# Holding back the first transposing DMA of a gated mixer kernel, and 256 more warm-up columns on TensorE

## The chip, the cores and the metric

The kernel runs on one core of a Trainium2 chip. Its time is the device time of one execution in microseconds (us); a kernel is compared with another by the medians of runs on the same chip. Separately, one execution is profiled. Its rows count from the start of the program's first instruction, so a row "at 5.61" starts 5.61 us into the span.

## The reference

Three results are computed from the same x (2048 tokens by 512) and mixed: an attention with 32 heads over 8 earlier tokens at distance 2, a mixer that works over the tokens (w1 and w2 multiply along the sequence), and a gate per token.

```python
qkv = x @ wqkv                          # 512 -> 3 x 512, 32 heads of 16
idx = pos[:, None] - 2 * arange(8)      # the 8 tokens that a token looks at
logits = einsum("bhsd,bhswd->bhsw", q, kg) / 4
a = (softmax(logits) . vg) @ wo
u = gelu(einsum("bsd,sf->bdf", layernorm(x), w1) + b1)    # f = 1792
b = (einsum("bdf,fs->bds", u, w2) + b2).transpose
g = sigmoid((x * gate_w).sum(-1))
out = g * a + (1 - g) * b
```

## The kernel before

The kernel lists its work as operations with an engine, an estimated duration and names that they read and write. A planner (`_Sched`, L72) puts them into one fixed order for each engine and works out which semaphores each must wait for. An operation in `deps` of another is waited for; one in `order` only comes ahead of it in the plan. SP issues nearly all loads, and an instruction that waits on SP holds back everything that stands behind it there. The field `lands` of a load is only an estimate that the planner orders by.

TensorE runs five stages in this order: the q, k and v projections (L617, four 128x512 matmuls for a tile of 128 columns by 512 tokens), with the attention logits' head sums between them (L696), the first half of the token mixer (L810), the second half (L860), and the output projection (L876). ScalarE takes the results out of PSUM (L625 and L628 for q, k and v), VectorE forms the attention products, the softmax and the weighted sums, and the last steps on VectorE (L897) mix the two branches before the result is stored.

The projections need x transposed. Its tokens are cut into four blocks of 512. Blocks 1 to 3 are transposed by DMAs (`ld_xt`, L457, issued at L460). Block 0 is brought in two ways, since the first matmuls wait for it:

- Columns 0 to 127 are loaded untransposed by a 128 KB load into the tile XP (`d_xp`, L479, issued by ScalarE at L429). Four small TensorE matmuls with an identity transpose them (`f_tr`, L540, matmuls at L544); ScalarE (L553) and VectorE (L555) each copy half of the result into the tile XT.
- Columns 128 to 511 are transposed by a DMA (`ld_xt0`, L470, issued by SP at L473).

The weights of q come in four 128 KB pieces, one for each 128 rows. The first, `d_wp0_0`, is issued by ScalarE behind `d_xp`; the other three, the two 256 KB halves of k's weights, the first rows of x and the transposing DMA of block 1 follow `ld_xt0` on SP. All this is the list `first_loads` (L481), whose dependences are cleared, so that none of these loads waits for anything in the kernel before.

The projections of block 0 are split into passes. First comes a pass over the first 128 rows for four banks of PSUM (four matmuls, needing the TensorE transposes and `d_wp0_0`), then a pass over the second 128 rows (needing `ld_xt0` and the second piece of q's weights), and so on (L633 to L639).

TensorE has nothing to do until then. It multiplies constants into a bank that is not read: five 512-column matmuls (warm1, L548), one of 256 columns (warm2), then the four transposes, then one of 512 columns (warm3, L552); all of them are the matmuls at L536. The first projection matmul is ordered behind warm3 (w3_, L639).

VectorE's first operation, `rp` (L426, instruction at L424), adds up columns of the identity that GpSimd makes at L417; its result is read by the head sums much later.

Of the kernel before, what the change touches and what calls it, by code (L numbers as in the profile page):

```python
# [333 lines left out]
def bass_gated_mix__sliding_local_dilated__mixer_token_mlp__prompt_kernel(nc, A_x, A_wqkv, A_wo, B_x, B_w1, B_b1, B_w2, B_b2, gate_w, out, dbg=None):  # L334
    with contextlib.ExitStack() as es:
# [79 lines left out]
        A = sch.add  # L415
# [7 lines left out]
            with nc.allow_low_precision(reason="exact 0/1 indicator sums"):  # L423
                return e.tensor_reduce(out=RP, in_=sub(IDENT, 0, [(4, 32), (1, 4)]), axis=AX.X, op=ALU.add)  # L424

        A("dve", f_rp, 0.2, reads=["ident"], writes=["rp"], name="rp")  # L426

        def mk_dma(dst, src):
            return lambda e: e.dma_start(dst, src)  # L429
# [3 lines left out]
        def throttle():  # L433
            return [init_dmas[-5]] if len(init_dmas) >= 5 else []

        def prev_dma():
            return [init_dmas[-1]] if init_dmas else []

        def ld_x(t0, n, q="sp"):
            ds = sch.dsem("x%d" % t0)  # L440
            op = sch.dma(q, mk_dma(X[:, t0:t0 + n, :], xv[:, t0:t0 + n, :]), n * 128 * D * 2, ds,
                         writes=["x%d" % t for t in range(t0, t0 + n)], deps=throttle() if q == "sp" else [], after=prev_dma() if q == "sp" else [], name="d_x%d" % t0)
            if q == "sp":
                init_dmas.append(op)
            return op

        def ld_w(tn, d0, n, q="sp"):
            ds = sch.dsem("wqkv%d_%d" % (tn, d0))
            op = sch.dma(q, mk_dma(WQKV[:, d0:d0 + n, tn * D:(tn + 1) * D], wqkv_v[:, d0:d0 + n, tn * D:(tn + 1) * D]),
                         n * 128 * D * 2, ds, writes=["wqkv%d_%d" % (tn, dt) for dt in range(d0, d0 + n)],  # L450
                         deps=throttle() if q == "sp" and n == 4 else [], after=prev_dma() if q == "sp" else [],
                         issue=0.65 if n == 4 else 0.45, name="d_wp%d_%d" % (tn, d0))
            if q == "sp":
                init_dmas.append(op)
            return op
# [11 lines left out]
        def xt_of(sb, d0=0, d1=4):  # L467
            return XT0[d0:d1] + (XT0[4:] if d0 == 0 else []) if sb == 0 else ["xt_%d" % t for t in range(4 * sb, 4 * sb + 4)]

        def ld_xt0():  # L470
            ds = sch.dsem("xt0")
            dst = XT[:, 1:4, 0:512]
            op = sch.dma("sp", lambda e: e.dma_start_transpose(dst, x2d[0:512, 128:512]), 512 * 384 * 2, ds, issue=1.25,  # L473
                         writes=XT0[1:4], after=prev_dma(), name="d_xt0")
            init_dmas.append(op)
            return op
# [4 lines left out]
        first_loads = [ld_w(0, 0, 1, "act"), ld_xt0(), ld_w(0, 1, 1), ld_w(0, 2, 1), ld_w(0, 3, 1), ld_w(1, 0, 2), ld_w(1, 2, 2),  # L481
                       ld_x(0, 2)]
        ld_xt(1)
        first_loads.append(init_dmas[-1])
        for op_, t_ in zip(first_loads, (3.4, 4.6, 5.0, 5.4, 5.8, 6.6, 7.4, 8.2, 10.6)):
            op_.lands = t_
            op_.deps.clear()
        d_xp.lands = 3.1
        first_loads[0].order.add(d_xp)
        init_dmas[:] = [first_loads[1]] + first_loads[5:]  # L490
        ld_x(2, 2)
        ld_x(4, 4)
# [7 lines left out]
        def ld_w1(j):  # L500
# [4 lines left out]
            if j < 4:  # L505
# [8 lines left out]
                       writes=["wo"], deps=throttle(), after=prev_dma(), name="d_wo")  # L514
# [4 lines left out]
        for i_, (v_, n_) in enumerate(((B_b1, NFT), (B_b2, NST))):  # L519
            vr = v_.rearrange("(t q j) -> q t j", q=4, j=32)  # L520
            for q_ in range(4):
                sch.dma("sp", mk_dma(psub(BR, 32 * q_, n_, 32 * i_, [(1, 32)]), vr[q_]), n_ * 64, ds_b, reads=["br"],
                        writes=["br_%d_%d" % (i_, q_)], deps=throttle(), after=prev_dma(), name="d_b_%d_%d" % (i_, q_), issue=0.45)
        d_w1.append(ld_w1(3))
        A("dve", lambda e: e.transpose(out=BT, in_=BR), 0.2, reads=["br_%d_%d" % (i_, q_) for i_ in range(2) for q_ in range(4)],
          writes=["btc"], name="t_b")
# [5 lines left out]
        def f_warm(n, w_=D):  # L532
            def fn(e):
                ins = None
                for _ in range(n):
                    ins = e.matmul(ps[:, 7, 0:w_], lhsT=CONE[:, 0:128], rhs=CONE[:, 0:w_], start=True, stop=True)  # L536
                return ins
            return fn

        def f_tr(h):  # L540
            def fn(e):
                ins = None
                for t in range(2):
                    ins = e.matmul(ps[:, 5 + h, 128 * t:128 * t + 128], lhsT=XP[:, 2 * h + t, :], rhs=IDENT, start=True, stop=True)  # L544
                return ins
            return fn
# [2 lines left out]
        w2_ = A("pe", f_warm(1, 256), 0.2, writes=["lg7_0", "lg7_1"], name="warm2", prio=-100)  # L549
        ta_ = A("pe", f_tr(0), 0.215, reads=["outs0", "ident"], writes=["lg5_0", "lg5_1"], after=[w2_], name="tr0", prio=-100)  # L550
        tr_ = A("pe", f_tr(1), 0.215, reads=["outs0", "ident"], writes=["lg6_0", "lg6_1"], after=[ta_], name="tr1", prio=-100)
        w3_ = A("pe", f_warm(1), 0.43, writes=["lg7_0", "lg7_1"], after=[tr_], name="warm3", prio=-100)  # L552
        A("act", lambda e: e.activation(out=XT[:, 0, 0:256], in_=ps[:, 5, 0:256], func=AF.Copy), 0.35, reads=["lg5_0", "lg5_1"],  # L553
          writes=["xt0_0"], name="ev_tra", prio=0)
        A("dve", lambda e: e.tensor_copy(out=XT[:, 0, 256:512], in_=ps[:, 6, 0:256]), 0.35, reads=["lg6_0", "lg6_1"],  # L555
          writes=["xt0_0b"], name="ev_trb", prio=0)
# [12 lines left out]
        for hf in range(2):  # L569
            t0 = 8 * hf  # L570
            for t in range(t0, t0 + 8):
                A("dve", (lambda t_: (lambda e: e.bn_stats(out=ST6[:, t_, :], in_=X[:, t_, :])))(t), 0.59,  # L572
                  reads=["x%d" % t], writes=["st6_%d" % t], name="ln1_%d" % t, prio=0)
# [13 lines left out]
              reads=["zc%d" % hf], writes=["sd%d" % hf], name="ln_sqrt%d" % hf, prio=0)  # L587
            A("dve", (lambda t0_: (lambda e: e.reciprocal(out=cols(RSTD, t0_, 8), in_=cols(SD, t0_, 8))))(t0), 0.25,
              reads=["sd%d" % hf], writes=["rstd%d" % hf], name="ln_rstd%d" % hf, prio=0)
# [43 lines left out]
        for (b0, d0, d1, s0, s1) in ((0, 0, 1, 0, 512), (0, 1, 2, 0, 512), (0, 2, 3, 0, 512), (0, 3, 4, 0, 512), (4, 0, 2, 0, 512), (4, 2, 4, 0, 512)):  # L633
            for b in range(b0, b0 + 4):
                tn, dl = first[b]
                last_main[0] = A("pe", f_proj(tn, dl, 0, b, d0, d1, s0, s1), 0.216 * (d1 - d0) * (s1 - s0) / 512,
                                 reads=xt_of(0, d0, d1) + ["wqkv%d_%d" % (tn, dt) for dt in range(d0, d1)],
                                 writes=fbn[b], after=[last_main[0]], name="pf_%s%d_%d_%d" % (tnames[tn], dl, d0, s0))
                last_main[0].order.add(w3_)  # L639
        for b, (tn, dl) in enumerate(first):  # L640
            A("act", f_evq(tn, dl, 0, b), 0.52, reads=fbn[b] + (["k5pad"] if tn == 1 else []),
              writes=["%s5_%d_0" % (tnames[tn], dl)], name="ev_%s%d_0" % (tnames[tn], dl), prio=0)
# [7 lines left out]
        for (tn, dl, sb) in seq_proj:  # L650
# [3 lines left out]
                             reads=xr + ["wqkv%d_%d" % (tn, dt) for dt in range(4)],  # L654
                             writes=["acc%d" % bank], after=[last_main[0]], name="pj_%s%d_%d" % (tnames[tn], dl, sb), prio=0)
            A("act", f_evq(tn, dl, sb, bank), 0.62, reads=["acc%d" % bank] + (["k5pad"] if tn == 1 else ["v5pad"] if tn == 2 else []),
              writes=["%s5_%d_%d" % (tnames[tn], dl, sb)], name="ev_%s%d_%d" % (tnames[tn], dl, sb), prio=0)
# [11 lines left out]
                writes=["xa"] + ["wqkv%d_%d" % (tn, dt) for tn in range(3) for dt in range(4)], name="d_xa")  # L669
        for t in range(NST):  # L670
# [5 lines left out]
          writes=["th"], name="g_tanh", prio=0)  # L676
        A("dve", lambda e: e.tensor_scalar(out=G, in0=TH, scalar1=0.5, scalar2=0.5, op0=ALU.mult, op1=ALU.add), 0.15,
          reads=["th"], writes=["g"], name="g_g", prio=0)
        A("dve", lambda e: e.tensor_scalar(out=OMG, in0=TH, scalar1=-0.5, scalar2=0.5, op0=ALU.mult, op1=ALU.add), 0.15,
          reads=["th"], writes=["omg"], name="g_omg", prio=0)  # L680
        A("dve", lambda e: e.tensor_tensor(out=C2, in0=OMG, in1=B2C, op=ALU.mult), 0.15,
          reads=["omg", "b2c"], writes=["c2"], name="g_c2", prio=0)
# [25 lines left out]
        for wh in range(2):  # L708
# [6 lines left out]
            for (dl, c0, nc_) in pieces:  # L715
# [3 lines left out]
                  reads=["q5_%d_%d" % (dl, sb) for sb in range(c0, c0 + nc_)] +  # L719
                        ["k5_%d_%d" % (dl, sb) for sb in range(max(c0 - 1, 0), c0 + nc_)] + ["k5pad"],  # L720
                  writes=wr, name="qkm_%d_%d_%d" % (wh, dl, c0), prio=0)
            rd = sum([pbn(b_) for b_ in bufs], []) + PBX[wh] + ["rp"]
            for wl in range(4):
                qop = A("pe", f_qkr(list(enumerate(bufs)), (wl,)), 0.92, reads=rd, writes=["lg%d_0" % (4 + wl), "lg%d_1" % (4 + wl)],
                        name="qkr_%d_%d" % (wh, wl), prio=-100 + wl, delay=BURST_DELAY)
                A("act", (lambda wh_, wl_: (lambda e: e.activation(out=ATT[:, :, 4 * wh_ + wl_, :], in_=ps[:, 4 + wl_, :].rearrange("p (h c) -> p h c", h=2), func=AF.Copy)))(wh, wl),  # L726
                  0.55, reads=["lg%d_0" % (4 + wl), "lg%d_1" % (4 + wl)], writes=["lw%d" % (4 * wh + wl)],
                  name="lev_%d_%d" % (wh, wl), prio=0)
# [24 lines left out]
        for hf in range(2):  # L753
# [3 lines left out]
              reads=["outs1"], writes=["lh%d" % hf] + (wall if hf == 0 else []), name="sm_sub%d" % hf, prio=0)  # L757
            if hf == 0:
                A("act", lambda e: e.activation(out=col(SD, 0), in_=col(ZC, 0), func=AF.Exp, scale=0.0), 1.5,
                  reads=["zc0"], writes=["sd0"], name="sm_pre")  # L760
            A("act", (lambda hf_, l_: (lambda e: e.activation(out=ATT[:, hf_], in_=l_, func=AF.Exp)))(hf, lgh), 1.95,  # L761
              reads=["lh%d" % hf], writes=["att%d" % hf], name="sm_exp%d" % hf, prio=0)
        for hf in range(2):
# [5 lines left out]
            def f_rcp(e, hf_=hf):  # L769
# [6 lines left out]
              reads=["rs%d" % hf], writes=["att%d" % hf], name="sm_nrm%d" % hf, prio=0)  # L776
# [4 lines left out]
        for u in range(8):  # L781
            c, hf = u // 2, u % 2
            ds_at = sch.dsem("atx%d" % u)
            for a_ in range(4):
                dst = bass.AP(ATX.tensor, ATX.offset + a_ * pst + u * NW * HC, [[4 * pst, 32], [1, NW * HC]])
                sch.dma("act", mk_dma(dst, psub(ATT, 32 * c, 32, hf * NW * HC, [(1, NW * HC)])), 32 * NW * HC * 2, ds_at, issue=0.62,
                        reads=["att%d" % hf], writes=["atx_%d_%d" % (u, a_)], deps=pb_readers, name="d_atx_%d_%d" % (u, a_))
        USEQ = [0, 2, 1, 3, 4, 6, 5, 7]
        for k_, u in enumerate(USEQ):
# [6 lines left out]
              reads=v_res + ["atx_%d_%d" % (u, a_) for a_ in range(4)], writes=[pn] + [qk_res, k_all][k_ % 2], name="avm_%d" % u)  # L796
            for (nm, n_, du) in (("ava", 4, 2.25), ("avb", 2, 1.2)):
                A("dve", (lambda pv_, n__: (lambda e: e.tensor_tensor(out=pv_[:, 0:n__], in0=pv_[:, 0:n__], in1=pv_[:, n__:2 * n__], op=ALU.add)))(pv, n_),  # L798
                  du, writes=[pn], name="%s_%d" % (nm, u))
# [27 lines left out]
        for ft in range(NFT):  # L827
# [5 lines left out]
              reads=["acc%d" % bank, "b1c"], writes=["ut%d" % ft] + ALLXT,  # L833
              name="gel_%d" % ft, prio=0)
# [84 lines left out]
        for i in range(NST):  # L919
# [4 lines left out]
            elif i > 1:  # L924
# [5 lines left out]
              reads=["acc%d" % bank, "omg", "c2"], writes=["t1_%d" % i, "x%d" % i],  # L930
              name="t1_%d" % i, prio=0)
# [119 lines left out]
```

## Time and profile before

| what | value |
|---|---|
| time, median of 3 runs | 168.18 us (167.72 to 168.53) |
| the profiled execution's own time | 168.55 us |
| its span, first to last instruction | 167.3 us |
| TensorE busy (matmuls) | 162.1 us, 97% of the span |
| VectorE busy | 151.3 us, 90% |
| ScalarE busy | 75.1 us, 45% |
| GpSimd busy | 0.7 us |
| mean DMA rate over the span | 177 GB/s |
| first projection matmul starts | 5.61 us |
| last matmul ends | about 165.1 us (L876) |

The profile names an engine's instructions by line: PE is TensorE, PEld its weight loads, DVE VectorE, ACT ScalarE, POOL GpSimd, SP the engine that issues loads. SPq and ACTq rows are DMA issues, and the time in such a row is how long the issue took, not the transfer. Queue q1 in the DMA view belongs to SP and q10 to ScalarE.

### The profile page before, as it was taken

The page shows a single profiled execution, that of the slowest core. Times are in us where ns is not written, and L with a number is a line of the kernel's source. Part 1 is how long each engine was busy: PE and PEld are TensorE (multiplying, and loading weights), DVE is VectorE, ACT ScalarE, POOL GpSimd, SP SyncE. Part 2 cuts the span into 40 slices and gives each one's busy share as a digit, 9 for nine tenths or more (in the row PEclk, how much of TensorE's full clock was granted, in tenths as well). Part 3 has the DMA queues.
Part 4 walks back from the last instruction along what each step waited for, and adds up shares of the span by engine and source line. Part 5 has one row for each costly group of instructions (what it writes and reads, how often), then busy time and mean ns, then how long its engine had stood idle before and what let it go on. Part 6 is the DMA issues. An engine that isn't in the chain of part 4 may idle for free.

```text
span 167.3 us, 2136 instructions
## 1 busy us (share of the span) xinstructions
PE 162.1 (97%) x845; PEld 77.5 (46%) x859; DVE 151.3 (90%) x154; ACT 75.1 (45%) x116; POOL 0.7 (0%) x8
## 2 busy tenths in 40 slices
PE   7699999999999999999999999999999999999994
PEld 2355555554454444444444444444444444444463
DVE  1055999999999999999999999999999999999896
ACT  3077688889899818793131121131231321310100
POOL 1000000000000000000000000000000000000000
PEclk9999999999999999999999999999999999999999
DMA  5999999959003846996779926462672570000454
GB/s 135 327 268 216 314 316 290 303 165 308 2 0 97 311 116 179 307 290 155 181 189 340 339 76 142 113 187 71 181 218 83 138 223 0 0 0 0 157 190 159
DMA packets 47625, 29.64 MB, mean 177 GB/s; under 512 B 9856, under 2 KB 46464, under 8 KB 47616
## 3 DMA queue, kind: packets, MB, share of 16 engines
q1 hardware_dynamic: 45120, 24.85, 54.4%
q10 hardware_dynamic: 2496, 4.66, 10.2%
q8 instruction: 7, 0.11, 0.3%
q14 instruction: 2, 0.02, 0.0%
HBM read 21.24 MB, written 2.10 MB: 140 GB/s over the span
## 4 chain that ended last, share of the span: by engine, by line
PE 91%; DMA 3%; DVE 2%; ACT 2%; issue 1%; ACTq 0%
PE ps L860 29%; PE ps L810 29%; PE ps L617 23%; PE ps L876 6%; PE ps L696 4%; DMA arena<-in_A_wqkv_dram 3%; DVE arena L897 2%; ACT L585 1%; ACT arena L628 1%; ACTq L429 0%; ACT arena L585 0%
## 5 line engine op out<-in xcount | busy, mean ns | idle before, releaser
L860 PE MATMUL ps<-arena 128*128 128x512 bf16 x220 | 48.5, 379 | 0.2
L810 PE MATMUL ps<-arena 128*128 128x512 bf16 x219 | 48.2, 379 | 0.4 <-issue 0.2
L617 PE MATMUL ps<-arena 128*128 128x512 bf16 x188 | 41.4, 379 | 1.6 <-DMA arena<-in_A_wqkv_dram 1.3
L688 DVE TENSOR_TENSOR arena<-arena 128x4096 bf16<-128x4096 bf16 (+1 forms) x12 | 35.5, 2998 | 2.5 <-ACT arena L628 2.1
L795 DVE TENSOR_TENSOR arena<-arena 128x8192 bf16<-128x8192 bf16 x8 | 35.0, 4419 | 0.0
L860 PEld LDWEIGHTS ps<-arena 128*128 128x128 bf16 x224 | 21.9, 98 | 26.4
L810 PEld LDWEIGHTS ps<-arena 128*128 128x128 bf16 x224 | 21.8, 98 | 26.6 <-ACT arena L726 0.4
L617 PEld LDWEIGHTS ps<-arena 128*128 128x128 bf16 x192 | 21.6, 113 | 21.5 <-issue 1.8
L928 ACT ACTIVATE arena<-ps,arena 128x512 bf16<-128x512 f32 x16 | 12.5, 778 | 39.4 <-PE ps L860 39.4
L798 DVE TENSOR_TENSOR arena<-arena 128x4096 bf16<-128x4096 bf16 (+1 forms) x16 | 27.0, 1751 | 0.0
L628 ACT ACTIVATE arena<-ps 128x512 bf16<-128x512 f32 x32 | 18.6, 596 | 4.5 <-PE ps L617 4.5
L831 ACT ACTIVATE arena<-ps,arena 128x512 bf16<-128x512 f32 x14 | 9.6, 687 | 22.2 <-PE ps L810 16.6
L572 DVE BATCH_NORM_STATS2 arena<-arena 128x6 f32<-128x512 bf16 x16 | 10.0, 682 | 6.1 <-DMA arena<-in_A_x_dram 6.1
L876 PE MATMUL ps<-arena 128*128 128x512 bf16 (+1 forms) x79 | 14.1, 336 | 0.1
L897 DVE SCALAR_TENSOR_TENSOR arena<-ps,arena 128x512 bf16<-128x512 f32 (+1 forms) x20 | 11.5, 637 | 0.9 <-PE ps L876 0.7
L596 ACT ACTIVATE arena<-arena 128x512 bf16<-128x512 bf16 x16 | 12.2, 804 | 0.0
L625 ACT ACTIVATE arena<-ps 128x512 bf16<-128x512 f32 x16 | 9.0, 597 | 6.2 <-PE ps L617 6.1
L876 PEld LDWEIGHTS ps<-arena 128*128 128x128 bf16 x80 | 7.8, 98 | 6.2
L672 DVE SCALAR_TENSOR_TENSOR arena<-arena 128x512 bf16<-128x512 bf16 x16 | 10.1, 689 | 0.0
L742 DVE TENSOR_TENSOR arena<-arena 128x512 bf16<-128x512 bf16 (+4 forms) x11 | 7.3, 667 | 0.6 <-ACT arena L761 0.2
L696 PE MATMUL ps<-arena 128*32 128x512 bf16 x128 | 7.3, 380 | 0.0
L726 ACT ACTIVATE arena<-ps 128x512 bf16<-128x512 f32 x8 | 4.7, 592 | 4.6 <-PE ps L696 4.6
(42 smaller groups left out, 40.0 us busy)
## 6 DMA issues: line engine op xcount, KB each, us to landing
arena<-in_B_w_dram SPq DMA_DIRECT2D x7, 1024.0 KB, 8.5
arena<-in_B_w_dram SPq DMA_DIRECT2D x8, 896.0 KB, 5.2
arena<-arena ACTq DMA_DIRECT2D x32, 128.0 KB, 2.9
arena<-in_A_x_dram SPq DMA_DIRECT2D x4, 512.0 KB, 6.1
out_dram<-arena SPq DMA_DIRECT2D x14, 128.0 KB, 1.7
arena<-in_A_x_dram SPq DMA_DIRECT2D x1, 1536.0 KB, 7.9
arena<-in_A_wqkv_dram SPq DMA_DIRECT2D x2, 256.0 KB, 3.8
arena<-in_A_x_dram SPq DMA_DIRECT2D x2, 256.0 KB, 3.6
```

What stands on the lines that cost most here:

```text
L596: A("act", (lambda t_: (lambda e: e.activation(out=X[:, t_, :], in_=X[:, t_, :], func=AF.Identity, scale=col(RSTD, t_), bias=col(NMR, t_)) ...
L617: ins = e.matmul(ps[:, bank, s0:s1], lhsT=lhsT, rhs=XT[:, dt, sb * 512 + s0:sb * 512 + s1], start=(dt == 0 and s0 == 0), stop=(dt == 3))
L628: return lambda e: e.activation(out=dst, in_=ps[:, bank, :], func=AF.Copy)
L688: return lambda e: e.tensor_tensor(out=PBL[buf][:, :, 512 * c0:512 * (c0 + nc_)], in0=in0, in1=in1, op=ALU.mult)
L696: ins = e.matmul(ps[32 * c:32 * c + 32, 4 + wl, :], lhsT=RP, rhs=PBL[buf][:, wl, c * 512:(c + 1) * 512], start=(dl == 0), stop=(dl == 3), ...
L795: A("dve", (lambda o_, i0, i1: (lambda e: e.tensor_tensor(out=o_, in0=i0, in1=i1, op=ALU.mult)))(pv, in0, in1), 4.4, reads=v_res + ["atx_% ...
L798: A("dve", (lambda pv_, n__: (lambda e: e.tensor_tensor(out=pv_[:, 0:n__], in0=pv_[:, 0:n__], in1=pv_[:, n__:2 * n__], op=ALU.add)))(pv, n ...
L810: ins = e.matmul(ps[:, bank, :], lhsT=W1W[:, slot, st, 128 * e_:128 * e_ + 128], rhs=X[:, st, :], start=(st == 0), stop=(st == NST - 1))
L860: ins = e.matmul(ps[:, bank, :], lhsT=W2S[slot][:, ft, 128 * e_:128 * e_ + 128], rhs=UT[:, ft, :], start=(ft == 0), stop=(ft == NFT - 1))
L876: ins = e.matmul(ps[:, bank, 0:c1 - c0], lhsT=OT[:, t, 128 * i:128 * i + 128], rhs=WO[:, t, c0:c1], start=(t == 0), stop=(t == 3))
L897: A("dve", (lambda i_, b_, c0_, c1_: (lambda e: e.scalar_tensor_tensor(out=T1[:, i_, c0_:c1_], in0=ps[:, b_, 0:c1_ - c0_], scalar=col(G, i ...
L928: A("act", (lambda i_, bank_: (lambda e: e.activation(out=T1[:, i_, :], in_=ps[:, bank_, :], func=AF.Identity, scale=col(OMG, i_), bias=co ...
```

## The change

Two things. The transposing DMA of block 0 (`first_loads[1]`) gets a dependence on `rp`, so SP waits with its first instruction until VectorE's first operation is done, and all of SP's later issues stand behind it. And one more constant matmul of 256 columns (warm4) comes behind warm3 on TensorE; the first projection matmul is now ordered behind warm4. The estimated landing times that the planner orders by are also raised. The planner's order on every engine stays the same apart from the new matmul, and the only new wait is SP's.

```diff
-        A("dve", f_rp, 0.2, reads=["ident"], writes=["rp"], name="rp")
+        c_rp = A("dve", f_rp, 0.2, reads=["ident"], writes=["rp"], name="rp")
...
-        for op_, t_ in zip(first_loads, (3.4, 4.6, 5.0, 5.4, 5.8, 6.6, 7.4, 8.2, 10.6)):
+        for op_, t_ in zip(first_loads, (3.5, 5.1, 5.5, 5.9, 6.3, 7.1, 7.9, 8.7, 11.1)):
             op_.lands = t_
             op_.deps.clear()
         d_xp.lands = 3.1
         first_loads[0].order.add(d_xp)
+        first_loads[1].deps.add(c_rp)
...
-        w3_ = A("pe", f_warm(1), 0.43, writes=["lg7_0", "lg7_1"], after=[tr_], name="warm3", prio=-100)
+        A("pe", f_warm(1), 0.43, writes=["lg7_0", "lg7_1"], after=[tr_], name="warm3", prio=-100)
+        w3_ = A("pe", f_warm(1, 256), 0.2, writes=["lg7_0", "lg7_1"], after=[tr_], name="warm4", prio=-100)
```

## Prediction

> **What bounds the kernel now.** I read the chain that ended last first. TensorE carries 91% of the span, and ahead of the first projection stands one DMA.
>
> ```profile
> PE 91%; DMA 3%; DVE 2%; ACT 2%; issue 1%; ACTq 0%
> ```
>
> The same chain in order of time, cut to its start, says which DMA, and that from 5.61 on matmuls follow one another:
>
> ```profile
> 0.80 0.46 ACTq L429
> 1.25 0.03 issue
> 1.28 4.24 DMA arena<-in_A_wqkv_dram
> 5.52 0.09 issue
> 5.61 8.36 PE ps L617 x38
> ```
>
> It is the 128 KB piece of q's weights that ScalarE issues at 1.28 (d_wp0_0). It lands at 5.52. A delay or gain here moves nearly everything behind it, since TensorE is 97% busy. Next the timeline of the first microseconds (start, duration, what; in brackets idle time and its releaser):
>
> ```profile
> 0.80 1.35 SPq L473 DMA_TRANSPOSE arena<-in_A_x_dram  x1
> ...
> 1.22 0.29 DVE L424 TENSOR_REDUCE arena<-arena 128x32 bf16<-128x128 bf16 x1 [1.22 <-POOL arena L417]
> ...
> 2.22 2.49 SPq L429 DMA_DIRECT2D arena<-in_A_wqkv_dram  x5
> ...
> 3.71 0.63 PE L536 MATMUL ps<-const-bfloat16-1.0 128*128 128x512 bf16 x1
> ...
> 3.96 0.42 DVE L555 CAST arena<-ps 128x256 bf16<-128x256 f32 x1 [2.45 <-PE ps L544]
> 4.75 0.47 SPq L429 DMA_DIRECT2D arena<-in_A_x_dram  x1
> 5.27 3.36 SPq L460 DMA_TRANSPOSE arena<-in_A_x_dram  x1
> ...
> 5.61 6.64 PE L617 MATMUL ps<-arena 128*128 128x512 bf16 x30 [1.26 <-DMA arena<-in_A_wqkv_dram]
> ```
>
> The other inputs of the first pass are ready by 3.96 + 0.42 = 4.38, so the weights are over a microsecond late. Why, the DMA view tells, cut to 2.85:3.45 (first row: queue, packets, MB, share of 16 engines) and to 3.45:4.70 (the other two):
>
> ```profile
> q1 hardware_dynamic: 677, 0.17, 128.4%
> ...
> q1 hardware_dynamic: 794, 0.25, 87.3%
> q10 hardware_dynamic: 144, 0.13, 33.6%
> ```
>
> From 2.85 to 3.45 only SP's queue moves anything: the transposing DMA, in 256-byte packets. ScalarE's weights, issued by 1.81, get their packets only after 3.45, beside the transposes. The load before them on that queue (XP, issued at 0.80) had its first packets at 2.08, 1.28 after its issue; the weights took 2.2. The transposing DMA went ahead of them.
>
> **The change part by part.**
>
> *The wait.* VectorE's first operation ends at 1.22 + 0.29 = 1.51. With 0.05 to be seen, as between SP's own neighbouring issues (2.16 to 2.22), SP issues at 1.56 instead of 0.80: 0.76 later. Behind it stand three pieces of q's weights (2.22 on), two of k's, x, then block 1's transposing DMA (5.27); each may be issued 0.76 later. VectorE and GpSimd wait for nothing new.
>
> *The weights of the first pass.* ScalarE's issue at 1.28 is now 0.28 ahead of SP's. With XP's 1.28 from issue to first packet they start at 2.56, behind XP on the same queue. In the packet rows XP's packets end at 2.82 before the change, a little sooner without SP's; 128 KB at the 289 GB/s of the 2.85:3.45 cut take 0.45, so they end near 3.2. XP landed 0.4 after its last packet; the weights 0.9 after theirs. So they land at 3.6 to 4.1. The first pass then waits for VectorE's copy, which ends at 4.38 (or 0.1 sooner, if XP lands sooner). With the 0.09 seen between landing and first matmul it starts near 4.45: 1.16 earlier. At a full clock its four matmuls take 4 x 0.216 (38 of them take 8.36 with pauses; two starts are 0.216 apart) and end issuing near 5.3.
>
> *The second pass* needs the transposing DMA and the second piece of q's weights, which now decide. In the kernel before these landed at 0.80 + 4.9 = 5.7 and 2.22 + 3.8 = 6.0, while TensorE was busy with the first pass until 5.61 + 0.86 = 6.47. After: the transposes' first packet was at 2.54, 1.74 after the issue, so now 1.56 + 1.74 = 3.30. Alone they run at 677 packets in 0.60 us; the 384 KB are 1,536 packets, 1.36 us, so the last is near 4.67. Before, beside the other queue, it was near 4.52. So the transposes end only about 0.15 later although they start 0.76 later, because the bytes that ran beside them have gone ahead. The weights behind them on SP are issued by 3.5 at the latest, well before the queue is free. Their landing moves by the same 0.15, to 6.13 from 5.98, and the second pass starts at 6.13 + 0.09 = 6.22 instead of 6.47: **0.25 earlier**.
>
> Bounds: the least delay is none with the four late parts of these landings gone (a load lands in 16 parts; in the trace 12 parts of the second piece were in by 5.51, the last at 5.98): 5.51 + 0.15 + 0.09 = 5.75, a gain of 0.72. The most is the whole 0.76: 5.98 + 0.76 + 0.09 = 6.83, a loss of 0.36. I take 0.15 because the packet rows show the 16 engines full in this stretch, so order is what changes and not how much is moved.
>
> *What comes after.* The third and later pieces landed at 6.2, 6.6, 7.5 and 8.2, and the passes that need them began at 7.34, 8.20, 9.06 and 10.79; even 0.76 more fits under all of them, tightest at the first: 6.22 + 0.76 + 0.09 = 7.07 against 7.34 - 0.25 = 7.09. Block 1 landed at 10.73 and is needed at 12.5. SP's block-1 issue took 3.36 against 1.35 for block 0, so it stood against a full queue; its end at 8.63 should move by the queue's 0.15 and not by 0.76. The first x rows land near 9.0 for VectorE, which idles 4.51 before them and 2.06 later before its first large product at 15.07; that product waits for ScalarE and so moves with TensorE. The chain then stays on TensorE, with VectorE released by it at the end (idle 0.72 at 157.35). So the 0.25 should reach the end.
>
> *warm4.* 256 columns at the slow clock of the warm-up (two 512-column warm-up loads start 0.43 apart) are 0.21; warm3 is issued at 3.71 and done issuing at 4.14, warm4 at 4.35. It lies under VectorE's copy until 4.38. Cost 0; were that cover gone, at most 0.21, and then still nothing while the second pass waits until 6.22. Below nothing it could only be worth something through the clock: the warm-up matmuls last 0.63, those of the projections 0.38.
>
> The Trainium skill, "TensorE: Matmul & The Clock Gate", section "What you observe" and what follows it, says the clock doubles after a busy window of about 3.4 us that runs free of the kernel's start. The trace agrees with the two speeds, 0.63 and 0.38; that the window can fall otherwise no trace here shows. By it the sum would be the same in the profiled run, where the first projection matmul is already fast.
>
> The sum: -0.25 + 0 = -0.25 on the profiled execution: 168.55 to 168.30 (span 167.3, about 1.25 around it). That execution is 0.37 above the median of 168.18, so against the median I put 168.18 - 0.25 = **167.9**. A measurement of this kernel can tell about 0.5%, 0.84 us, from no change, and this forecast lies within it.
>
> **The rivals.**
>
> A, *SP's delay is carried through* (slower than before). If the second piece of q's weights is bound by its issue and not by the queue, it lands at 6.74 and TensorE starts the second pass at 6.83: +0.36, 168.5. It decides as soon as that landing moves by more than 6.47 - 0.09 - 5.98 = 0.40. Against it: q1 is full from 2.85 to 4.70. For it: that piece's first packets came at 4.37, 2.15 after its issue; were all of that latency and none of it queue, they would now come at 5.13 and not at 4.67. 0.15.
>
> B, *the late parts vanish.* 5.75 for the second pass: -0.72, 167.5. For it: the first pieces' last four parts are late exactly where two queues shared. Against it: SP's later pieces have late parts too. 0.17.
>
> C, *nothing is won*, as the weights still come behind the transposes, or beside them, because their descriptors are made late: first pass near 5.6 and second at 6.5, 168.2. For it: they waited 2.2 once. Against it: XP, issued in the same moment as the transposes, was not held back. 0.13.
>
> D, *the clock.* TensorE is idle 4.14 to 5.61 before. If in some executions the fast clock comes after that hole only, one more 3.4 us window later (4.5 + 3.4 = 7.9), matmuls from 5.61 to 7.9 run at half speed: a loss of 1.1 in the kernel before, which the change (idle only 5.3 to 6.2) would save: 168.18 - 0.25 - 1.1 = 166.8. The page named above is the source of that window. Against it: the four times shown lie within 0.83 and the profiled one, with a fast first pass, is the slowest of them. 0.07.
>
> **How the numbers follow.** Forecast 0.43 (gain 0.1 to 0.4), A 0.15, B 0.17, C 0.13, D 0.07, something unseen that costs over 0.84 us, such as A with a late clock, 0.05. Range: from B with 0.2 of spread between medians to A with as much, 167.3 to 168.7, which leaves out D and the unseen. Faster by over 0.5% (below 167.34): D and a third of B, 0.13. Slower by over 0.5%: 0.06, the unseen and a sliver of A. Within: 0.81.
>
> **What would show it.** Right: SP's first issue near 1.56; ScalarE's weights landed by 4.1; first L617 near 4.45, then a pause of about 0.9 on TensorE before the fifth L617 matmul near 6.2; the rest of the chain as before, 0.25 earlier. Wrong: the fifth matmul after 6.47 (A), a first matmul near 5.6 (C), no pause behind the fourth (B), 0.63 us matmuls at L617 (the clock), or a new wait for x or block 1 later on TensorE.

## The result and the profile after

The changed kernel is a little slower: median 168.66 us against 168.49 us of before over 19 runs of each, and a ratio of 1.0033 (95% interval 1.0019 to 1.0048), that is about +0.56 us. Five runs of before (170.3 to 171.8) and one of the changed kernel (193.8), none of them profiled, are left out of that ratio as disturbed. Two later measurements of the same changed kernel gave 1.0036 (1.0003 to 1.0069) and 1.0035 (1.0013 to 1.0056). It is within 0.5% of no change, as the chances had it, but on the other side: 0.25 us less was forecast. The profiled execution took 168.48, its span is 167.2 (before: 168.55 and 167.3).

The page's chain by engine, changed kernel; SP and a longer DVE share are new in it:

```profile
PE 92%; DVE 3%; DMA 2%; issue 1%; SPq 1%; POOL 0%; POOLq 0%
```

The same chain in order of time (start, duration, what):

```profile
0.88 0.30 POOL arena L417
1.19 0.02 issue
1.21 0.30 DVE arena L424
1.51 0.02 issue
1.52 1.35 SPq L473
2.87 0.06 issue
2.93 3.34 DMA arena<-in_A_wqkv_dram
6.27 0.14 issue
6.40 7.29 PE ps L619 x33
```

Before, the chain went through ScalarE's first weights. Now it goes through the new wait itself: GpSimd's identity, VectorE's first operation, SP's transposing issue, and behind it on SP the second piece of q's weights (issued at 2.93, landed at 6.27). The timeline of the changed kernel shows the other side of the exchange:

```profile
3.70 0.84 PE L537 MATMUL ps<-const-bfloat16-1.0 128*128 128x512 bf16 x2
...
3.94 0.42 DVE L557 CAST arena<-ps 128x256 bf16<-128x256 f32 x1 [2.45 <-PE ps L545]
...
4.42 1.36 PE L619 MATMUL ps<-arena 128*128 128x512 bf16 x4
...
5.98 4.01 SPq L460 DMA_TRANSPOSE arena<-in_A_x_dram  x1
...
6.40 8.80 PE L619 MATMUL ps<-arena 128*128 128x512 bf16 x39 [0.61 <-DMA arena<-in_A_wqkv_dram]
...
10.23 1.29 DVE L574 BATCH_NORM_STATS2 arena<-arena 128x6 f32<-128x512 bf16 x2 [5.86 <-DMA arena<-in_A_x_dram]
```

The first projection pass starts at 4.42 instead of 5.61, 1.19 earlier, as intended and as forecast. But its four matmuls take 1.36 (4 x 0.216 to issue was forecast, which with the end of the last is 1.02), since the first two still run at the slow clock (0.61 and 0.52 instead of 0.38). They end into a pause, and the fifth starts at 6.40. In the profiled execution of before the fifth started at 6.47. So 1.19 won at the first matmul is 0.07 at the fifth, and 0.07 is the whole difference of the two profiled times (168.55 and 168.48). These two executions alone don't show the loss of 0.56.

The DMA view, cut to the two stretches of the prediction (2.85:3.45 the first two rows, 3.45:4.70 the last two), shows what became of the full DMA engines:

```profile
q1 hardware_dynamic: 190, 0.05, 34.4%
q10 hardware_dynamic: 79, 0.07, 32.8%
...
q1 hardware_dynamic: 943, 0.24, 120.0%
q10 hardware_dynamic: 26, 0.02, 5.4%
```

The same view gives the rates: 194 and 212 GB/s, where before it was 289 and 308. Over the 1.85 us that is 0.38 MB instead of 0.56. The weights have gone ahead, but the transposing DMA doesn't make use of the room: its 943 packets take 1.25 us, while before 677 of them took 0.60.

### The profile page after: what moved, and what is told of

It reads as the page before. It is cut to its first block, busy times and chain, and to the rows that moved or that the text cites. A ratio compares the mean times of both kernels' runs of the same rounds, so it can differ in the third digit from the quotient of the medians.

```text
span 167.2 us, 2138 instructions
## 1 busy us (share of the span) xinstructions
PE 162.6 (97%) x846; PEld 77.7 (46%) x860; DVE 151.3 (90%) x154; ACT 75.0 (45%) x116; POOL 0.7 (0%) x8
## 4 chain that ended last, share of the span: by engine, by line
PE 92%; DVE 3%; DMA 2%; issue 1%; SPq 1%; POOL 0%; POOLq 0%
PE ps L862 29%; PE ps L812 29%; PE ps L619 24%; PE ps L878 6%; PE ps L698 4%; DVE arena L899 2%; DMA arena<-in_A_wqkv_dram 2%; SPq L473 1%; POOL arena L417 0%; DVE arena L424 0%; POOLq L417 0%; POOLq L1038 0%
```

## The experiments

Two theories stood against each other at the outset. Theory 1: the loss comes at the start, and all of it from SP's wait; the profiled execution of before was not a usual one. Theory 2: the added matmul or something later makes the loss. Each row is one profiled execution; "fifth" is the start of the fifth projection matmul, that is of the second pass, in that profile, and "weights 2" the landing of the second piece of q's weights.

| kernel | SP's first issue | first pass starts | weights 2 | fifth | time of the profiled run | ratio to before (95%) |
|---|---|---|---|---|---|---|
| before | 0.80 | 5.61 | 5.98 | 6.47 | 168.55 | |
| before, once more | 0.80 | 4.67 | 5.49 | 6.12 | 169.10 | 0.9984 (0.9950 to 1.0017) |
| before, a third time | 0.80 | 5.25 | 5.72 | 6.11 | 168.19 | 1.0024 (0.9973 to 1.0075) |
| 256 columns alone | 0.80 | 4.70 | 5.59 | 5.98 | 168.06 | 0.9987 (0.9951 to 1.0024) |
| wait for the identity | 1.21 | 4.47 | 6.03 | 6.16 | 168.27 | 1.0006 (0.9978 to 1.0034) |
| changed | 1.52 | 4.42 | 6.27 | 6.40 | 168.48 | 1.0033 (1.0019 to 1.0048) |
| changed, once more | 1.53 | 4.58 | 7.17 | 7.30 | 171.08 | 1.0036 (1.0003 to 1.0069) |
| changed, a third time | 1.53 | 4.52 | 6.29 | 6.42 | 168.51 | 1.0035 (1.0013 to 1.0056) |
| wait alone | 1.53 | 4.49 | 6.89 | 7.02 | 169.21 | 1.0052 (1.0015 to 1.0088) |
| wait for XP's landing | 3.18 | 4.40 | 7.88 | 8.02 | 171.76 | 1.0186 (1.0129 to 1.0244) |

In six of these ten rows the time less the fifth is 162.08 to 162.11, in a seventh 162.19. Whatever TensorE does before the fifth projection matmul, the rest of the kernel takes the same in these seven. The other three are told below. In the four rows without a wait the fifth starts 0.22 after the fourth, as matmuls do that follow one another at the full clock: the first pass decides. In the six with a wait it starts 0.13 to 0.14 after the landing of weights 2, and 0.48 to 2.40 after the fourth: the weights decide.

**The kernel before, profiled again** (no edit).

> The kernel before, profiled once more. Theory 1 (start order): the profiled execution of before was not its usual one; in executions of 167.7 to 167.9 ScalarE's weights get their packets before the transposes are through, the second projection pass (fifth L617 matmul) starts near 5.7 instead of 6.47, and the time is about 0.7 lower than 168.5. So a profile with a time of 167.7 to 168.0 shows the fifth L617 matmul at 5.6 to 5.9, and one with 168.5 shows it near 6.47. Theory 2 (TensorE): the start is the same in every execution (fifth matmul at 6.4 to 6.5) and the spread of 0.8 lies elsewhere, so a profile near 167.8 differs later in the span. Ratio to before: 1.000 either way.

Its chain, cut to where it joins TensorE, and TensorE's own row at the start:

```profile
15.66 4.97 DMA arena<-in_A_x_dram
20.63 0.14 issue
20.76 18.30 PE ps L617 x84
```

```profile
4.67 2.69 PE L617 MATMUL ps<-arena 128*128 128x512 bf16 x9 [0.41 <-DMA arena<-in_A_wqkv_dram]
```

Half right. The first pass started 0.94 earlier than in the first profile, since ScalarE's weights landed at 4.58 and not at 5.52, and the second pass 0.35 earlier. That the second pass won less has a cause of its own: three of the first pass's four matmuls ran at the slow clock (0.59, 0.63 and 0.58), so the fifth started only 1.45 after the first, not 0.86 as in the first profile. But the time was 169.10 and not 167.7 to 168.0: the transposing DMA of a later block landed only at 20.63 and TensorE stood for it, 0.9 us that no other of these profiles has. The third profile (below) has the early start without that.

**SP's wait alone.**

```diff
-        A("pe", f_warm(1), 0.43, writes=["lg7_0", "lg7_1"], after=[tr_], name="warm3", prio=-100)
-        w3_ = A("pe", f_warm(1, 256), 0.2, writes=["lg7_0", "lg7_1"], after=[tr_], name="warm4", prio=-100)
+        w3_ = A("pe", f_warm(1), 0.43, writes=["lg7_0", "lg7_1"], after=[tr_], name="warm3", prio=-100)
```

> SP's wait for VectorE's first operation, without the added matmul. Theory 1: all of the loss comes from the wait, so the ratio is that of the whole change, 1.002 to 1.005 (168.5 to 168.8), with the fifth L617 matmul near 6.4. Theory 2: the wait costs nothing and the ratio is 0.999 to 1.001.

```profile
1.53 1.34 SPq L473
2.88 0.06 issue
2.93 3.96 DMA arena<-in_A_wqkv_dram
6.89 0.14 issue
7.02 32.11 PE ps L618 x148
```

Ratio 1.0052 (1.0015 to 1.0088): the wait alone loses no less than the whole change. Its chain is that of the changed kernel, and the weights took 3.96 from issue to landing in this execution, 0.6 more than in the changed kernel's profile above: three of the 16 parts in which a load lands came at 6.69 to 6.89, the other 13 by 6.24.

**The 256 columns alone** (the changed kernel without the line `first_loads[1].deps.add(c_rp)` and with the old estimates).

> The added matmul of 256 columns, without SP's wait. Theory 1: it lies under VectorE's copy and costs nothing, ratio 0.999 to 1.001, most times 167.7 to 168.0 as in before. Theory 2: it carries the loss, ratio 1.002 to 1.005.

```profile
1.28 3.33 DMA arena<-in_A_wqkv_dram
4.61 0.09 issue
4.70 9.44 PE ps L618 x41
```

Ratio 0.9987 (0.9951 to 1.0024): no cost that shows. The chain stays on ScalarE's weights and there is no pause behind the first pass. Theory 2 falls with these two.

**A shorter wait.**

```diff
-        first_loads[1].deps.add(c_rp)
+        first_loads[1].deps.add(c_ident)
```

> The whole change, but SP waits for GpSimd's identity (done at about 1.18) and not for VectorE's first operation (1.51), so it issues about 0.33 earlier than in the changed kernel. Theory 1: if the whole delay of SP counts, the fifth L617 matmul comes near 6.05 and the time is about 0.33 lower than that of the changed kernel, near 168.3; if only the order of the two queues counts, about the same as the changed kernel, 168.6. Theory 2: 168.6, as the added matmul is still there.

```profile
4.59 1.47 PE ps L619 x4
6.06 0.10 issue
6.16 32.15 PE ps L619 x148
```

SP issues at 1.21, 0.41 later than before. The chain runs through the first pass (4.59 to 6.06) and not through SP; the weights landed at 6.03, just before that pass was done. But matmuls overlap (at the full clock they last 0.38 and start 0.22 apart): the fourth started at 5.68 and the fifth 0.48 later, 0.13 after the landing, so here too it waited for the weights. What this delay costs stays open. The ratio is 1.0006 (0.9978 to 1.0034), an interval that holds no cost as well as the changed kernel's 1.0033. But the median is 168.54, against 168.17 of before measured beside it, and the fastest run 168.27, against 167.71; the profiled execution is that fastest run. So the time of theory 1 (near 168.3) was met in the profile alone, and the landing is what this run shows.

**A longer wait.**

```diff
-        first_loads[1].deps.add(c_rp)
+        first_loads[1].deps.add(d_xp)
```

> The changed kernel, but SP waits until the load of XP has landed (about 3.15), so it issues near 3.2 instead of 1.52. Theory 1 (SP's delay is carried through in full): in the profiles so far the second piece of q's weights landed 4.7 to 4.8 after SP's first issue (5.49 and 5.59 after 0.80, 6.03 after 1.21, 6.27 after 1.52), so now near 7.95; fifth L617-pass matmul near 8.05, time near 8.05 + 162.1 = 170.2. Theory 2 (only the order of the two queues counts, the full DMA engines make up for a later issue): landing near 6.5, time near 168.7.

The weights landed at 7.88 and the fifth came at 8.02, as theory 1 had it; the time is 1.6 higher than it gave, which the next point explains. This run also has the transposing DMA with nothing beside it, since both of ScalarE's loads are done by then. Its packets by half microseconds, from 4.55, 5.05 and 5.55 on (the DMA view of that kernel):

```profile
q1 hardware_dynamic: 398, 0.10, 86.4%
...
q1 hardware_dynamic: 407, 0.10, 110.7%
...
q1 hardware_dynamic: 497, 0.13, 121.5%
```

The 1,536 packets run from 4.56 to 6.48, 1.92 us. Beside ScalarE's weights, in the kernel before, they ran from 2.54 to 4.52, 1.98 us. Being alone gained them next to nothing in this execution.

**The changed kernel again, and TensorE's clock** (no edit).

> The changed kernel once more. Theory 1: ratio 1.002 to 1.005; in the profile the second piece of q's weights lands 6.2 to 6.9 and the time is the start of the fifth projection matmul plus 162.1. Theory 2: the same ratio, without that sum holding.

The ratio is as expected. The profiled execution was one of 171.08, the slowest of its twelve; its weights landed later than expected, and the sum with 162.1 does not hold. The busy time by stretch of that kernel (length, then busy time of PE, PEld, DVE, ACT and POOL with their counts, the granted clock, DMA share, GB/s):

```profile
4.00:7.39 3.39, 1.38 (x7) 0.49 (x6) 0.23 (x1) 0.00 (x0) 0.00 (x0) 1.00 1.02 262
7.40:10.80 3.40, 3.40 (x9) 1.19 (x9) 0.63 (x2) 0.00 (x0) 0.00 (x0) 0.50 1.20 280
10.82:14.00 3.18, 3.18 (x17) 1.63 (x15) 1.58 (x4) 2.13 (x5) 0.00 (x0) 1.00 1.05 286
```

and its TensorE rows:

```profile
4.58 1.02 PE L619 MATMUL ps<-arena 128*128 128x512 bf16 x4 [0.32 <-DMA arena<-in_A_wqkv_dram]
7.30 0.96 PE L619 MATMUL ps<-arena 128*128 128x512 bf16 x2 [1.69 <-DMA arena<-in_A_wqkv_dram]
```

The weights landed at 7.17. TensorE stood idle for 1.69 between the passes, and the granted clock fell to 0.50 from 7.40 to 10.81; nine matmuls ran in a time that has room for sixteen. Half of 3.41 is 1.7, and time less the fifth is 163.78, 1.7 more than elsewhere. The longer wait above shows the same (idle for 2.02, clock at 0.50 from 8.97 to 12.38, time less the fifth 163.74). The Trainium skill, "TensorE: Matmul & The Clock Gate", section "Why this matters for your kernels", warns of TensorE idle for more than about 3 us. Here 1.69 was enough, in a stretch of 3.4 with 1.38 busy, and the measurement decides.

**The transposing DMA cut in two** (no wait, 256 columns kept; SP issues columns 128 to 255, then the second piece of weights, then columns 256 to 511).

```diff
-            dst = XT[:, 1:4, 0:512]
-            op = sch.dma("sp", lambda e: e.dma_start_transpose(dst, x2d[0:512, 128:512]), 512 * 384 * 2, ds, issue=1.25,
+            dst = XT[:, d0:d1, 0:512]
+            op = sch.dma("sp", lambda e: e.dma_start_transpose(dst, x2d[0:512, 128 * d0:128 * d1]), 512 * 128 * (d1 - d0) * 2, ds, issue=0.42 * (d1 - d0),
...
-        first_loads = [ld_w(0, 0, 1, "act"), ld_xt0(), ld_w(0, 1, 1), ld_w(0, 2, 1),
+        first_loads = [ld_w(0, 0, 1, "act"), ld_xt0(1, 2), ld_w(0, 1, 1), ld_xt0(2, 4), ld_w(0, 2, 1),
```

> No wait on SP, the added 256 columns kept, and block 0's transposing DMA cut in two: SP issues columns 128 to 255 first, then the second piece of q's weights, then columns 256 to 511, then the rest as before. Theory 1 (the second pass waits for what SP issues first): a third of the packets stands ahead of the weights, 0.45 instead of 1.36 at 677 packets in 0.60 us, so both inputs of the second pass land near 4.6, the second pass follows the first without a pause at 5.4 to 6.1, by the clock of the first pass's matmuls, and the time is 167.5 to 168.2, at or under before. Theory 2 (only the order of the two queues counts): no change to before, or slower by the 0.5 of one more DMA issue on SP, 168.2 to 168.7.

```profile
0.80 1.23 SPq L473
...
2.09 0.56 SPq L429
...
2.71 1.25 SPq L473
...
4.00 3.70 DMA arena<-in_A_wqkv_dram
7.70 0.14 issue
7.83 31.32 PE ps L618 x144
```

Slower, 1.0030 (1.0003 to 1.0058). The second pass did start early, at 5.71, though the weights landed at 5.57 and not near 4.6. But the issue of a third of the columns took SP 1.23, and that of two thirds 1.25, where all three together take 1.35. The second such issue pushes every later one back (that of the third piece of q's weights stands at 4.00, before at 2.83), and the third pass, at 7.83 in the chain, waits for its weights, which landed at 7.70 (in the first profile of before, it began at 7.34). In this execution the cut that was to take packets out of the way lost more on SP's issues than it won.

**The kernel before, a third profile** (no edit).

> The kernel before, one more profile. Theory 1: time = start of the fifth projection matmul + 162.1, unless TensorE waits for x later on; in most executions that start is 5.6 to 6.1 and the first piece of q's weights lands near 4.6, not 5.5 as in the first profile. Theory 2: the start is 6.4 to 6.5 as in the first profile.

```profile
1.28 3.88 DMA arena<-in_A_wqkv_dram
5.16 0.09 issue
5.25 8.80 PE ps L617 x40
```

ScalarE's weights at 5.16, the fifth at 6.11, the time 168.19 = 6.11 + 162.08. So before's start does vary from execution to execution, through that one landing: 4.58, 5.16 and 5.52 in its three profiles. The fifth varies less (6.12, 6.11 and 6.47): the start at 4.67 met the slow clock, that at 5.25 no longer did (four matmuls of 0.38).

**The second piece of weights issued by ScalarE**, in the kernel before, in that kernel with the 256 columns, and in the changed kernel.

```diff
-        first_loads = [ld_w(0, 0, 1, "act"), ld_xt0(), ld_w(0, 1, 1), ld_w(0, 2, 1),
+        first_loads = [ld_w(0, 0, 1, "act"), ld_xt0(), ld_w(0, 1, 1, "act"), ld_w(0, 2, 1),
...
+        first_loads[2].order.add(first_loads[0])
```

> The kernel before, with the second piece of q's weights issued by ScalarE behind the first instead of by SP behind the transposing DMA. Theory 1 (the transposing DMA takes about 2.0 us of packets whatever runs beside it, and what SP issues behind it comes later by that): the weights no longer stand behind the transposes, so the second pass waits for the transposes alone (landed at 5.05 to 5.74 in four profiles of the issue at 0.80) and SP's later issues come 0.56 earlier; fifth projection matmul 5.3 to 6.1, time 167.6 to 168.2, at or under before by 0.2 to 0.4. Theory 2 (the 16 DMA engines are full, so only bytes count): the same bytes stand ahead of the second pass, no change, 168.2 to 168.4.

> The same with the added 256 columns on TensorE. Theory 1: as without them, 167.6 to 168.2, since they lie ahead of the first pass's inputs. Theory 2: as before, 168.2 to 168.4.

> The changed kernel, SP's wait and the 256 columns included, with the second piece of q's weights issued by ScalarE. Theory 1: the second pass waits for the transposes alone, which start 1.5 after SP's issue at 1.52 and land at 5.87 as in the profile of the changed kernel: fifth projection matmul near 6.0, time near 168.1, half a microsecond under the changed kernel, and still 0.3 to 0.5 over the same kernel without SP's wait. Theory 2: no difference to the changed kernel, 168.7 to 169.0.

Theory 1's gain doesn't show. The ratios are 1.0000 (0.9986 to 1.0015), 0.9987 (0.9961 to 1.0014) and 1.0039 (1.0022 to 1.0055): issuing the weights from the other engine is worth nothing that can be measured, with the wait or without it. In the profiles they landed at 6.01, 5.71 and 5.25 from ScalarE, the transposes at 5.79, 5.12 and 5.97, and the fifth came at 6.53, 5.85 and 6.01: in the first later than the 5.3 to 6.1 of theory 1. With the wait it is then the transposing DMA itself that the second pass waits for in the profiled execution; the chain of the third kernel says so:

```profile
1.52 4.44 DMA arena<-in_A_x_dram
6.01 7.31 PE ps L620 x33
```

So it isn't only what stands behind the transposing DMA on SP: the DMA's own landing is late too. This execution, with its fifth at 6.01 and a time of 168.20, is just what theory 1 gave, but it was the fastest of twelve with a median of 168.87. Where the others lose those 0.67 us no profile shows; that stays open. None of the three beats before by more than the measurement can tell.

**The changed kernel, a third profile** (no edit).

> The changed kernel, one more profile. The theory as it stands now: in the kernel before the second pass starts when the first is done, since the second piece of q's weights landed 0.4 to 0.6 ahead of that in four profiles (5.49 to 5.98); SP's wait moves that landing by its whole 0.72, to 6.2 at the least and up to 7.2 when its last parts are late, past the end of the first pass. So here the fifth projection matmul starts 0.13 after that landing, with a pause before it, and the time is that start plus 162.1 (168.4 to 169.3), or 1.7 more if TensorE's clock drops in the pause. Rival: the second pass follows the first without a pause, at 5.4 to 6.2, and the time over before comes from later in the span.

```profile
4.64 1.70 PE ps L619 x4
6.34 0.08 issue
6.42 7.72 PE ps L619 x35
```

The start and the sum hold (weights at 6.29, fifth at 6.42, 168.51 = 6.42 + 162.09), and the pause is hidden in the chain: the first pass ran at the slow clock here, 1.70 in the chain for four matmuls, and was done only at 6.34, after the landing. Its fourth matmul started at 5.78, though, and the fifth came 0.64 later.

## Why the prediction was wrong

*Right.* SP issued at 1.52 (forecast 1.56); the first pass started at 4.42 (4.45), released by VectorE's copy; the 256 columns cost nothing that shows; the rest of the kernel follows the second pass without loss or gain. Block 1 and the later loads were not waited for in the profiled execution. ScalarE's weights came later than forecast (4.30, not 3.6 to 4.1) and were covered only because the copy ended at 4.36.

*Wrong: the step "the transposes end only about 0.15 later although they start 0.76 later, because the bytes that ran beside them have gone ahead".* The second piece of weights lands 3.3 after its issue in the changed kernel, 3.4 with the shorter wait, 3.3 with the longer one, 3.3 and 3.5 in two profiles of before: SP's delay is carried through in full. Where the last parts were late it took longer, 4.0 and 4.2 in two executions with the wait. The first profile of before has 3.8, because its last four parts were late, so the 0.29 between its landing (5.98) and that of the changed kernel (6.27) hides most of the true 0.72. The step rested on a rate, 677 packets in 0.60 us, read off a stretch in which the DMA was running at its fastest, and on the DMA engines being full. Alone, the same DMA takes 1.92 and not 1.36.

*Wrong: what the second pass was waiting for.* The prediction saw that the first pass of before ended 0.4 after the inputs of the second were there, and took that as something to be won. In the profiles with SP at 0.80, the landing plus 0.13 was 0.36, 0.50, 0.26 and 0.26 ahead of the fifth matmul. That is slack for SP's queue: a delay of 0.41 about used it up (fifth at 6.16, as in the mean of before), one of 0.72 overdraws it by 0.2 to 0.5. By the profiles, the mean fifth is 6.17 without the wait (four of them) and 6.61 with it at 1.52 (three, without the one of 7.30): +0.44, or +0.61 with it, against +0.56 from the ratio. An earlier first pass gains at most that slack, as the second has another input.

*Mis-sized: the first pass itself, "at a full clock".* Moved to 4.42, it started while TensorE's clock was still slow and took 1.36; in the changed kernel's third profile 1.82 (4.52 to 6.34), and 1.02 only in the second, which started at 4.58. In before's first profile all its matmuls, from 5.61 on, were at 0.38. The prediction said that no trace shows the rise of the clock at another time; these do. With the wait this cost nothing, as the weights came later still. Without it, it is part of what an early start loses: in before's second profile the fifth came 1.45 after a first matmul at 4.67, in the other two 0.86 after one at 5.25 and at 5.61.

*Rival A* is what happened. Its condition (the landing moves by more than 0.40) holds against before's landings without late parts (5.49 to 5.72, then 6.27), though not against the 5.98 of the first profile; its price was +0.36 in the forecast, +0.56 measured. It was given 0.15, because "q1 is full from 2.85 to 4.70" spoke against it. That row tells how long packets were under way, not that more could not have been moved: in the changed kernel it shows 120.0% at two thirds of the rate.

*Rival B* had the late parts vanish. They come and go: in the kernel before's first profile, in the wait alone, in one profile of the changed kernel. *Rival C*: ScalarE's weights did come early. *Rival D* gave the change a gain by a shorter pause of TensorE. No profile without the wait shows the late clock that it needs: matmuls of 0.38 began by 5.90 in each. The runs with a wait show the reverse: the pause moves behind the first pass, and where it reached 1.69 the clock fell, which cost 1.7 us.

*The base.* The sum started from one execution, whose first weights landed at 5.52. Before's other two profiles have 4.58 and 5.16, so what the change was to win was partly there already.

What stays open is what sets the pace of the transposing DMA (1.9 to 2.5 from first packet to last, alone or not), why the rate falls where it stands beside ScalarE's weights, why some parts of a landing are late in some executions, and what sets the moment at which TensorE's clock rises.

## What to carry to other kernels

A load that is late isn't worth more than the distance to the next input that its consumer needs: before a queue is held back to let another one through, read the landing of everything that stands behind it, over more than one profiled execution, and compare its slack with the delay. A DMA view that is busy in every slice doesn't show that a transfer could go faster once it is alone; time from issue to landing, over several executions, is the safer row. A pause of TensorE costs more than its length when it takes the clock along, and a pass that is moved forward may meet a clock that has not risen yet.

## What the runs showed of the hardware

- The granted clock fell to 0.50 after one idle stretch of 1.69 us, and after one of 2.02, for 3.41 us each.
- TensorE's clock rose at different moments: the first projection matmul took 0.59 to 0.62 us in seven of the ten profiles of the table and 0.38 in three, where it started at 4.58, 5.25 and 5.61; the last slow one ended at 6.34.
- The first transposing DMA's issue cost SP about the same for three sizes: 1.23 for 128 columns, 1.25 for 256, 1.35 for 384 (512 rows each). A later one, of 512 columns and behind other loads, took 3.36.
- A transposing DMA's 1,536 packets of 256 bytes took 1.92 us alone and 1.98 beside a 128 KB load.
